# A mixture-of-experts kernel: each expert step branches to one of two product widths, and the overflow branch stands before the first expert

## The chip, the cores and the metric

One core of one Trainium2 chip runs the whole program as a single launch. The metric is the device time of that launch in microseconds (us), and lower is better. Before the change the median of three runs is 975.46 us (975.08 to 977.14).

Engine names are those of the profile: PE is TensorE (matmuls; PEld its weight loads), DVE is VectorE, ACT is ScalarE, POOL is GpSimd, SP is the engine that issues nearly all DMAs.

## What is computed

Three stages follow each other. Only the second is touched by the change, and the start of the third.

```python
x = attention(q, k, v, s)                      # 4 batches, 8 heads, 576 tokens, head size 64 -> x is 2304 x 512
expert = argmax(normed(x) @ normed(emb).T)     # 8 experts
for e in range(8):                             # hidden size 1024
    m = expert == e
    out[m] = gate[m] * (relu(x[m] @ w1[e]) @ w2[e])
y = ((out @ w_a) * (out @ w_b)) @ w_out        # hidden size 1536
```

How many tokens an expert gets depends on the data. All matmuls are made from two parts, a rounded high part and the remainder, so that each product is three matmuls: high by high, low by high, high by low.

## The kernel before, in words

**Attention and routing** (to 260 us of the span). The tokens are scattered by expert into the DRAM tensor `xs`, and the counts are put into a small integer tile `ci`: row 0 the start of each slot, row 1 its count, row 2 the largest excess of a count over the slot's capacity, row 3 the expert that has the slot. Slot 0 is expert 0, slots 1 to 7 the others by falling count. The capacities are fixed: `CAPS = [352, 368, 344, 328, 296, 288, 288, 272]`.

**The expert loop** (267 to 510 us): eight slots `e`, eight steps `f` each. A step takes 128 of the 1024 hidden units. `hmm(e, f)` makes 12 matmuls into a PSUM bank `h` (4 blocks of the model width, 3 parts each); ACT takes the relu and rounds it (`hh`, L1415), DVE makes the remainder (`hl`, L1416). `ymm(e, f)` makes 12 matmuls from `hh` and `hl` into four banks `y`. All of them have `CAPS[e]` columns, whatever the count is. PE runs `hmm` of a step, then `ymm` of the step before, so that ACT and DVE have the length of two groups for `hh` and `hl`. After the last step `y` is copied to SBUF (L173 on ACT, L171 on DVE) and written to `yt`.

Between the steps the same loop issues, in program order:

- `xload(e)`, `xtr(e, d)`: a slot's tokens are loaded and transposed on PE (L1281), rounded on ACT (L1284), the remainder on DVE (L1285);
- `wload2()`, `wsplit2()`: the next expert's weights, 512 KB a load through three staging buffers (SP, L228), rounded on ACT (L258), the remainders on DVE and POOL, one half each (L266). A buffer is free again when both halves are done;
- `zfill(e)`: zeros behind a slot's tokens (SP, L1138); it needs the slot's count in a register of SP (L1259);
- `misc`: five small pieces of the gate's softmax, with two loads of ACT's function table (L1362, L1372);
- in the last expert `tick()`: the third stage's weights, which come as 64-bit numbers, are decoded: on ACT L240, on DVE L241, L248 and L251; then rounded on ACT (L1351) and the remainder made on POOL (L1353). One tick a step, eight in all; the decoding goes on in the third stage.

**Overflow**: if a count is over its capacity, a loop over experts computes the rest in plain fp32. It stands in `tc.If(most > 0)` (L1531), placed before slot 1; `most` is read from `ci` into a register of every engine (L1595) after step 2 of slot 0. Tile closes its hand-written order there and opens it again behind it.

**The third stage** (from 504 us): `abmm`, `omm`; its first items run while the last `ymm` is still open.

The order of the instructions on each engine is the program's order here, by `tc.manual_schedule()`. The engines wait for each other by semaphores alone.

## Time and profile before

| what | value |
|---|---|
| median of 3 runs | 975.46 us |
| the profiled execution | 968.9 us, span of its instructions 967.2 us |
| PE busy | 940.4 us, 97% |
| DVE, ACT, POOL busy | 492.7, 427.8, 337.0 us |
| moved by DMA | 123.30 MB |
| mean granted clock of PE | 0.990 |

The span runs from the first to the last instruction; 1.7 us of the profiled execution lie outside it. Times in rows are microseconds from the start of the span unless "ns" is said. A matmul's record is longer than the distance to the next one, since matmuls overlap in the array; the pace of PE is read from the distance of starts. L-numbers are lines of the kernel before.

### The profile page before, as it was taken

The numbers are of one execution on the slowest core, as the hardware profiler recorded it, in microseconds if no ns is written. First come the engines' busy times: TensorE is split into PE (matmuls) and PEld (weight loads), VectorE is DVE, ScalarE is ACT, GpSimd is POOL, SyncE is SP. The second block draws the span as 40 slices with busy tenths as digits, with TensorE's granted clock in tenths as the row PEclk, the third lists the DMA queues.
The fourth block names the chain that finished last, engine by engine and source line by source line (L and its number), as shares of the span: only waits on it lengthen the run. The fifth ranks groups of instructions, "written<-read, shape, count | busy, mean of one in ns | idle before, by whom it ended". The sixth has DMA issues, their size and how long they took to land.

```text
span 967.2 us, 17807 instructions
## 1 busy us (share of the span) xinstructions
PE 940.4 (97%) x6430; PEld 860.7 (89%) x6431; DVE 492.7 (51%) x1269; ACT 427.8 (44%) x1064; POOL 337.0 (35%) x460
## 2 busy tenths in 40 slices
PE   8999999999799999999999999999999999999996
PEld 7787787877599999999998999999999999999995
DVE  6678787786744433444498888633222222222111
ACT  4588787877463544555454444421211111111111
POOL 8566556579232333334343444552001001001001
PEclk9999999999999999999999999999999999999998
DMA  6789797885285767676575444203010010000000
GB/s 177 191 189 236 177 240 195 186 232 161 91 243 189 214 191 206 204 227 182 181 227 170 156 130 118 80 1 99 1 33 34 1 33 34 1 1 33 1 1 34
DMA packets 107637, 123.30 MB, mean 127 GB/s; under 512 B 59161, under 2 KB 73449, under 8 KB 107545
## 3 DMA queue, kind: packets, MB, share of 16 engines
q1 hardware_dynamic: 103609, 112.37, 41.9%
q0 software_dynamic: 3616, 9.48, 2.7%
q8 instruction: 52, 0.85, 0.4%
q14 instruction: 40, 0.33, 0.1%
q10 hardware_dynamic: 320, 0.27, 0.1%
HBM read 86.58 MB, written 19.92 MB: 110 GB/s over the span
## 4 chain that ended last, share of the span: by engine, by line
issue 32%; PE 26%; DVE 3%; POOL 3%; DMA 2%; ACT 0%; POOLq 0%; SPq 0%; DVEq 0%; ACTq 0%
PE h L1409 9%; PE y L1429 8%; PE h L1469 3%; PE x L1469 3%; PE y L1490 2%; POOL out_dram L1508 1%; POOL pm L1392 1%; DVE cv L248 1%; DMA pm<-pd,pos 1%; DVE cv L251 1%; PE x L1281 1%; DMA st<-in_moe_w_b_dram 0%; PE x L1490 0%; PE h L1490 0%; DVE xl L1457 0%
## 5 line engine op out<-in xcount | busy, mean ns | idle before, releaser
L1480 DVE TENSOR_TENSOR mx<-x,mx 128x384 f32<-128x384 f32 x72 | 40.0, 556 | 222.1 <-PE x L1469 222.0
L1508 POOL DMA_INDIRECT out_dram<-mx,pmt x18 | 17.7, 984 | 290.0 <-DVE mx L1507 221.2
L1481 ACT CAST hh<-mx 128x384 fp32r<-128x384 f32 x71 | 36.4, 513 | 160.5 <-DVE mx L1480 160.5
L1475 ACT COPY mx<-h 128x384 f32<-128x384 f32 x72 | 34.5, 479 | 145.1 <-PE h L1469 145.1
L572 POOL TENSOR_SCALAR bt<-ck,cumc 128x192 f32<-128x192 f32 (+3 forms) x128 | 74.0, 589 | 62.2 <-DVE mn L646 29.5
L652 ACT ACTIVATE z<-z,mn 128x192 f32<-128x192 f32 (+3 forms) x128 | 78.5, 614 | 28.9 <-DVE mn L646 26.4
L1469 PE MATMUL h<-xh,w 128*128 128x384 f32 x288 | 79.8, 337 | 1.0 <-ACT mx L1475 1.0
L1469 PE MATMUL h<-xh,v 128*128 128x384 f32 x288 | 79.7, 337 | 0.0
L1469 PE MATMUL x<-xh,w 128*128 128x384 f32 x288 | 79.0, 334 | 0.0
L266 POOL TENSOR_TENSOR w<-st,w 128x512 fp32r<-128x512 f32 (+1 forms) x41 | 44.1, 1088 | 72.9 <-ACT w L258 55.9
L266 POOL TENSOR_TENSOR v<-st,v 128x512 fp32r<-128x512 f32 x32 | 42.6, 1331 | 73.2 <-ACT v L258 65.7
L646 DVE CUSTOM_DVE_ANT_0 z<-st,bt 128x192 f32<-128x192 f32 (+3 forms) x128 | 59.2, 477 | 16.3 <-PE st L635 11.5
L739 PE MATMUL pt<-ident,z 128*128 128x128 f32 x448 | 65.3, 280 | 1.1 <-DVE ql L385 0.6
L783 PE MATMUL xa<-pT,vn 128*64 128x128 f32 x896 | 65.7, 282 | 0.6
L632 PE MATMUL st<-KS,QS 128*128 128x288 f32 (+3 forms) x160 | 59.6, 378 | 4.8 <-DVE mn L646 2.3
L1409 PE MATMUL h<-xh,w 128*128 128x352 f32 (+3 forms) x256 | 63.3, 316 | 0.0
L1482 DVE TENSOR_TENSOR hl<-mx,hh 128x384 fp32r<-128x384 f32 x71 | 41.0, 577 | 41.1 <-ACT hh L1481 41.1
L1429 PE MATMUL y<-hh,w 128*128 128x352 f32 (+3 forms) x256 | 61.6, 309 | 0.0
L1409 PE MATMUL h<-xh,v 128*128 128x368 f32 (+3 forms) x256 | 61.2, 310 | 0.0
L783 PEld LDWEIGHTS xa<-pT,vn 128*64 128x64 f32 x896 | 47.3, 136 | 14.8 <-issue 5.3
L1429 PE MATMUL y<-hh,v 128*128 128x368 f32 (+3 forms) x256 | 60.1, 306 | 0.0
L1490 PE MATMUL y<-v,hh 128*128 128x512 f32 x192 | 59.8, 392 | 0.0
(286 smaller groups left out, 2545.7 us busy)
## 6 DMA issues: line engine op xcount, KB each, us to landing
st<-in_moe_w_dram SPq DMA_DIRECT2D x64, 512.0 KB, 3.9
ck<-cumd SPq DMA_DIRECT2D x16, 576.0 KB, 5.8
QS<-sp SPq DMA_DIRECT2D x56, 128.0 KB, 4.7
st<-in_moe_w_a_dram SPq DMA_DIRECT2D x12, 512.0 KB, 3.8
st<-in_moe_w_b_dram SPq DMA_DIRECT2D x12, 512.0 KB, 3.6
st<-in_moe_w_out_dram SPq DMA_DIRECT2D x12, 512.0 KB, 3.7
xg<-yt SPq DMA_DIRECT2D x6, 768.0 KB
xg<-xs SPq DMA_DIRECT2D x8, 512.0 KB, 4.8
```

The source lines that it names most:

```text
L266: e.tensor_tensor(out=o[:, 1, a:b], in0=t[:, a:b], in1=o[:, 0, a:b].bitcast(F32), op=ALU.subtract)
L572: nc.gpsimd.tensor_scalar(out=bt[:m, h, :kk], in0=cks[u][:m, h, :kk], scalar1=-1.0, scalar2=cumc[:m, c - 1, hh:hh + 1], op0=ALU.mult, op1= ...
L632: nc.tensor.matmul(st[:m, :wp], lhsT=qs[:, h, s0 - 64:s0 - 64 + m], rhs=ks[:, h, c0:c0 + wp], start=True, stop=False)
L646: nc.vector.tensor_tensor_reduce(out=z[:m, h, c0:c0 + w], in0=st[:m, :w], in1=bt[:m, h, c0:c0 + w], op0=ALU.add, op1=ALU.min, scale=1.0, s ...
L652: nc.scalar.activation(out=z[:m, h, :kk], in_=z[:m, h, :kk], func=AF.Exp, scale=-1.0, bias=m1, accum_out=rsum[:m, tid(b, c), 2 * p + h:2 * ...
L739: nc.tensor.transpose(out=pt[:, 128 * x:128 * x + 128], in_=zs[i][:, h, a0:a0 + 128] if c else z0s[u % 2], identity=ident)
L783: nc.tensor.matmul(xa[64 * h:64 * h + 64, :m], lhsT=v_[:m, 2 * p + h, :], rhs=locs[i][bk, h], start=bk == 0, stop=bk == c,)
L1409: nc.tensor.matmul(ph[:, :CAPS[e]], lhsT=w[:, hl, 128 * f:128 * f + 128], rhs=mv[:, d, :], start=k_ == 0, stop=k_ == 11,)
L1429: nc.tensor.matmul(ys[e][d][:, :CAPS[e]], lhsT=w[:, hl, c0 + 128 * d:c0 + 128 * d + 128], rhs=mv, start=f == 0 and k_ == 0, stop=f == 7 an ...
L1469: nc.tensor.matmul(p, lhsT=w[:, hl, d, c0:c0 + 128], rhs=mv[:, d, :], start=d == 0 and k_ == 0, stop=d == 3 and k_ == 2,)
L1482: nc.vector.tensor_tensor(out=gl, in0=g, in1=gh.bitcast(F32), op=ALU.subtract)
L1490: nc.tensor.matmul(ots[i][t], lhsT=st[:, 128 * t:128 * t + 128], rhs=w[:, hl, c0:c0 + 512], start=f == 0 and k_ == 0, stop=f == 11 and k_ ...
```

## The change

1. A slot has two widths: `ARMS`. PE reads the slot's count into a register (`count`, one load a slot), and every step is now one `tc.If` with two arms, the same 24 matmuls once with the narrow and once with the wide width. `hmm` of a step and `ymm` of the step before stand in the same arm; at a slot's first step and behind its last there is an `If` of 12 matmuls each: nine branches a slot, 72 in all. ACT and DVE go on working on `CAPS[e]` columns.
2. The PSUM banks `h` and `y` are allocated once, not for each step.
3. The overflow branch stands before slot 0, between the load of its tokens and the first `zfill`; its tiles are other buffers, and `w2` is read in halves. The register loads for `zfill(1)` are ahead of it.
4. In the last expert the ticks of steps 4 and 6 are left out, and the remainders of the first six decoded pieces are made on DVE, not on POOL.

```diff
+ARMS = [[288, 352], [352, 368], [336, 344], [312, 328], [280, 296], [256, 288], [256, 288], [256, 272]]
...
-                r = nc.sync.value_load(ci[:1, 1, e:e + 1], min_val=0, max_val=N)
+                r = cbase[e] if e in cbase else nc.sync.value_load(ci[:1, 1, e:e + 1], min_val=0, max_val=N)
...
-                e = nc.gpsimd
+                e = nc.vector if x < 6 else nc.gpsimd
...
+            def count(e):
+                cnts[e] = nc.tensor.value_load(ci[:1, 1, e:e + 1], min_val=0, max_val=N)
+
+            def narrow(e, body):
...
+                    m = len(arms) // 2
+                    with tc.If(cnts[e] < arms[m - 1] + 1) as cmp:
+                        tree(arms[:m])
+                    with cmp.Else():
+                        tree(arms[m:])
...
+                    def both(n):
+                        mm(n)
+                        mm2(n)
+
+                    narrow(e, both)
+                    rest()
...
             xload(0)
+            cbase[1] = nc.sync.value_load(ci[:1, 1, 1:2], min_val=0, max_val=N)
+            who(1)
...
+            for x in range(WARM[2]):
+                warm((hb + yb)[x % 6], w[:, :128], w[:, :512], 1)
+            count(0)
+            most = nc.values_load(ci[:1, 2, 0:1], min_val=-CAP, max_val=N)
+            overflow()
             zfill(1)
...
-                if e == 1:
-                    sched.close()
-                    overflow()
-                    sched.enter_context(tc.manual_schedule())
                 for f in range(8):
-                    hmm(e, f)
-                    if (e, f) == (0, 2):
-                        most = nc.values_load(ci[:1, 2, 0:1], min_val=-CAP, max_val=N)
-                    if prev:
-                        ymm(*prev)
+                    if f == 5 and e + 1 < E:
+                        count(e + 1)
+                    products(e, f, prev)
...
-                        for _ in range(TICKS[0]):
+                        for _ in range(TICKS[0] if f not in (4, 6) else 0):
                             tick()
...
-                    ymm(*prev)
+                    finish(prev)
```

**The order on PE, last expert.** `h` and `y` are PSUM banks, `xh`, `hh` and `hl` the halves of tokens and hidden units, `v` weights. Before, one step follows the other:

```order
L1429 MATMUL y_7779<-hh,v_7575 128x272
L1429 MATMUL y_7779<-hl,v_7575 128x272
L1429 MATMUL y_7779<-hh,v_7575 128x272
L1409 MATMUL h_7804<-xh,v_7413 128x272
L1409 MATMUL h_7804<-xl,v_7413 128x272
```

In the change, the end of the narrow arm of a step, and the start of its wide arm:

```order
L1456 MATMUL y_4965<-hh,v_9020 128x256
L1456 MATMUL y_4965<-hl,v_9020 128x256
L1456 MATMUL y_4965<-hh,v_9020 128x256
L1415 UNCONDITIONAL_BRANCH
L1431 MATMUL h_4960<-xh,v_8625 128x272
L1431 MATMUL h_4960<-xl,v_8625 128x272
```

and the end of that wide arm, with the next step behind it:

```order
L1456 MATMUL y_4965<-hh,v_9020 128x272
L1456 MATMUL y_4965<-hl,v_9020 128x272
L1456 MATMUL y_4965<-hh,v_9020 128x272
L1415 UNCONDITIONAL_BRANCH
L1415 COMPARE_AND_BRANCH
L1431 MATMUL h_4961<-xh,v_8625 128x256
L1431 MATMUL h_4961<-xl,v_8625 128x256
```

The narrow arm comes first, and its last instruction jumps over the 24 matmuls of the wide one. No wait is added at the branches. The other four engines have one unconditional branch for each `If` and nothing else.

**The order on SP, from the load of slot 0's tokens (`xg<-xs`) on.** Before:

```order
L1266 DMA xg<-xs 128x2x512
L1267 DMA xg<-xs 96x512
L1259 TENSOR_LOAD ci
L1259 ISA x2
L1254 TENSOR_LOAD ci
L1254 ISA x2
L1434 TENSOR_LOAD ci
L1434 ISA x2
L1138 ISA
L1138 DMA xs<-zrow 736x1x256
L228 DMA st<-in_moe_w_dram 128x2x512
```

In the change, up to the branch, and from the branch's end:

```order
L1267 DMA xg<-xs 128x2x512
L1268 DMA xg<-xs 96x512
L1627 TENSOR_LOAD ci
L1627 ISA x2
L1255 TENSOR_LOAD ci
L1255 ISA x2
L1635 TENSOR_LOAD ci
L1635 ISA x2
L1580 COMPARE_AND_BRANCH
...
L1580 UNCONDITIONAL_BRANCH
L1139 ISA
L1139 DMA xs<-zrow 736x1x256
```

The number of register loads ahead of the zero fill is the same, three; the branch, with its waits for what SP has issued so far, stands between them and the zero fill, and so ahead of the first weight load.

**The order on DVE, last expert, steps 3 to 5.** `hl` and `xl` are remainders, `cv` the decoded piece, `st` the staging buffer. Before:

```order
L1416 SCALAR_TENSOR_TENSOR hl<-h_7842,hh 128x272
L1457 TENSOR_TENSOR xl<-xg,xh 128x384
L241 TENSOR_SCALAR st_7794<-st_7794 128x512
L248 SCALAR_TENSOR_TENSOR cv<-cv,st_7794 128x512
L251 SCALAR_TENSOR_TENSOR cv<-st_7794,cv 128x512
L1416 SCALAR_TENSOR_TENSOR hl<-h_7885,hh 128x272
L1457 TENSOR_TENSOR xl<-xg,xh 128x384
L241 TENSOR_SCALAR st_7833<-st_7833 128x512
L248 SCALAR_TENSOR_TENSOR cv<-cv,st_7833 128x512
L251 SCALAR_TENSOR_TENSOR cv<-st_7833,cv 128x512
L1416 SCALAR_TENSOR_TENSOR hl<-h_7925,hh 128x272
```

In the change:

```order
L1440 SCALAR_TENSOR_TENSOR hl<-h_4961,hh 128x272
L1508 TENSOR_TENSOR xl<-xg,xh 128x384
L242 TENSOR_SCALAR st_9224<-st_9224 128x512
L1415 UNCONDITIONAL_BRANCH
L1354 TENSOR_TENSOR w_9358<-cv,w_9358 128x512
L249 SCALAR_TENSOR_TENSOR cv<-cv,st_9224 128x512
L252 SCALAR_TENSOR_TENSOR cv<-st_9224,cv 128x512
L1440 SCALAR_TENSOR_TENSOR hl<-h_4960,hh 128x272
L1508 TENSOR_TENSOR xl<-xg,xh 128x384
L1415 UNCONDITIONAL_BRANCH
L1440 SCALAR_TENSOR_TENSOR hl<-h_4961,hh 128x272
```

A tick has one DVE operation more (L1354, the remainder that POOL made), and every second step from step 4 on has no tick.

## Rows read from the trace of the kernel before

**Rows 1.** The page, busy time: share of the span, then instructions.

```profile
PE 940.4 (97%) x6430; PEld 860.7 (89%) x6431; DVE 492.7 (51%) x1269; ACT 427.8 (44%) x1064; POOL 337.0 (35%) x460
```

**Rows 2.** Windows: stretch, length, busy PE, PEld, DVE, ACT, POOL, PE clock, DMA share, GB/s.

```profile
260.00:265.00 5.00, 3.10 (x11) 2.19 (x10) 4.39 (x10) 0.00 (x0) 0.00 (x0) 0.84 0.48 158
265.00:270.00 5.00, 5.00 (x26) 4.74 (x26) 2.04 (x4) 1.84 (x5) 0.00 (x0) 0.67 0.62 125
...
400.00:450.00 50.00, 50.00 (x364) 48.34 (x364) 21.45 (x39) 24.94 (x53) 18.46 (x14) 1.00 0.72 211
```

**Rows 3.** Timeline of PE: start, length, what [idle before and who ended it].

```profile
264.85 2.70 PE L1281 MATMUL y<-ident,xg 128*128 128x128 f32 x12 [1.90 <-DMA xg<-xs]
...
301.79 0.40 PE L1429 MATMUL y<-hl,w 128*128 128x352 f32 x1 [0.30 <-PEq L1531]
...
499.56 0.39 PE L1429 MATMUL y<-hl,v 128*128 128x272 f32 x1 [0.33 <-DVE hl L1416]
...
503.15 0.39 PE L1429 MATMUL y<-hl,v 128*128 128x272 f32 x1 [0.32 <-DVE hl L1416]
...
517.75 0.44 PE L1469 MATMUL h<-xh,w 128*128 128x384 f32 x1 [0.98 <-ACT mx L1475]
```

**Rows 4.** Timeline of PE: firsts of two neighbouring groups of 12 matmuls, two widths.

```profile
298.68 0.33 PE L1409 MATMUL h<-xh,v 128*128 128x368 f32 x1
...
300.69 0.32 PE L1429 MATMUL y<-hh,w 128*128 128x352 f32 x1
...
494.41 0.28 PE L1409 MATMUL h<-xh,v 128*128 128x272 f32 x1
...
495.91 0.29 PE L1429 MATMUL y<-hh,v 128*128 128x272 f32 x1
```

**Rows 5.** Line L1531, the overflow branch (q: an engine's queue).

```profile
L1531 SPq EVENT_SEMAPHORE  x9: 17/17/17, 298.8 to 302.1; - x9
...
L1531 PEldq COMPARE_BRANCH  x1: 357/357/357, 299.1 to 299.1; - x1
```

**Rows 6.** Timeline of PEld: the last weight load ahead of the overflow branch, the first behind.

```profile
300.85 0.34 PEld L1429 LDWEIGHTS y<-hh,w 128*128 128x128 f32 x2
301.75 0.19 PEld L1429 LDWEIGHTS y<-hl,w 128*128 128x128 f32 x1 [0.56 <-issue]
```

**Rows 7.** Line L1595, a register load on PE.

```profile
L1595 PEldq TENSOR_LOAD <-ci x1: 488/488/488, 272.7 to 272.7; - x1
```

**Rows 8.** Groups by line and shape: the shortest matmuls in a row.

```profile
L167 PE MATMUL xa<-ones 128*128 128x128 bf16 x130 | 9.3, 241 | 1.3 <-DVE ones L1068 1.3
```

**Rows 9.** Timeline of ACT, slot 0.

```profile
273.28 1.14 ACT L258 CAST w<-st 128x512 fp32r<-128x512 f32 x2 [2.85 <-DMA st<-in_moe_w_dram]
...
280.62 1.14 ACT L258 CAST v<-st 128x512 fp32r<-128x512 f32 x2 [2.12 <-DMA st<-in_moe_w_dram]
281.78 1.28 ACT L1362 ACT_TABLE_LOAD   x1
...
283.20 0.45 ACT L1415 ACTIVATE hh<-h 128x352 fp32r<-128x352 f32 x1
```

**Rows 10.** Timeline of DVE: slot 0, then the last expert.

```profile
283.73 0.47 DVE L1416 SCALAR_TENSOR_TENSOR hl<-h,hh 128x352 fp32r<-128x352 f32 x1
...
288.12 0.68 DVE L266 TENSOR_TENSOR v<-st,v 128x512 fp32r<-128x512 f32 x1
...
500.41 1.60 DVE L248 SCALAR_TENSOR_TENSOR cv<-cv,st 128x512 uint32<-128x512 uint32 x1
502.05 0.69 DVE L251 SCALAR_TENSOR_TENSOR cv<-st,cv 128x512 uint32<-128x512 uint32 x1
```

**Rows 11.** Timeline of POOL, last expert.

```profile
499.93 1.53 POOL L1353 TENSOR_TENSOR w<-cv,w 128x512 fp32r<-128x512 f32 x1 [2.06 <-issue]
```

**Rows 12.** DMA: queue, packets, MB, share of 16 engines; issue, KB, us to landing.

```profile
q8 instruction: 52, 0.85, 0.4%
...
z<-in_moe_expert_emb_dram POOLq DMA_DIRECT2D x1, 16.0 KB, 2.3
```

More of the change, by code (lines that the diff above doesn't have):

```diff
@@ L1402, in hmm @@
             def hmm(e, f):
[L1403 removed]
+                ph = hb[f % 2]
                 xh, xl = xhs[e]
[L1405 to L1413 removed]
@@ L1414, in hmm, with mm @@
-                hh, hl_ = (hp.tile([128, GT], F32R, name=x)[:, :CAPS[e]] for x in ("hh", "hl"))
-                nc.scalar.activation(out=hh, in_=ph[:, :CAPS[e]], func=AF.Relu)
-                nc.vector.scalar_tensor_tensor(
-                    out=hl_, in0=ph[:, :CAPS[e]], scalar=0.0, in1=hh.bitcast(F32), op0=ALU.max, op1=ALU.subtract
-                )
-                hs[e, f] = (hh, hl_)
+                def mm(n):
+                    k_ = 0
+                    for d in range(4):
+                        w = slots[e, d]
+                        for hl, mv in ((0, xh), (0, xl), (1, xh)):
+                            nc.tensor.matmul(
+                                ph[:, :n], lhsT=w[:, hl, 128 * f:128 * f + 128], rhs=mv[:, d, :n],
+                                start=k_ == 0, stop=k_ == 11,
+                            )
+                            k_ += 1
@@ L1524, in overflow @@
             def overflow():
[L1526 to L1529 removed]
+                xo, xT, *hT = (mxp.tile([128, 512], F32, name="mx") for _ in range(4))
+                w = tmp.tile([128, 512], F32, name="cv").rearrange("p (k c) -> p k c", k=4)
                 po, py = bank("x"), bank("x")
@@ L1572, in overflow @@
-                            nc.vector.tensor_copy(out=yo, in_=py)
+                                for x in range(2):
+                                    nc.sync.dma_start(
+                                        out=w,
+                                        in_=w2[bass.ds(pe, 1), 512 * x:512 * x + 512, 128 * d:128 * d + 128].rearrange("a (k p) c -> p (a k) c", p=128),
+                                    )
+                                    for f in range(4):
+                                        nc.tensor.matmul(
+                                            py[:, 128 * d:128 * d + 128], lhsT=w[:, f, :], rhs=hT[x][:, 128 * f:128 * f + 128],
+                                            start=x + f == 0, stop=x + f == 4,
+                                        )
@@ L1579, in moe_kernel @@
+            who(1)
+            w = slots[0, 0][:, 0, :]
+            hb = [ps.tile([128, 512], F32, name="h%d" % x) for x in range(2)]
+            yb = [ps.tile([128, 512], F32, name="y%d" % x) for x in range(4)]
+            for x in range(WARM[2]):
[3 more added lines that the diff above has]
+            overflow()
             zfill(1)
```

86 lines of the change are left out of this document (44 added, 42 removed).

## Prediction

> **What bounds the kernel now.** I read the page first: PE is busy for 97% of the span [rows 1]. Then the windows, to see where that is not so: PE waits around 255 to 265 us, ahead of the expert loop, and its clock is granted at 0.84 and 0.67 in the windows there [rows 2], which is partly the lower of its two levels, 1.2 GHz; at 400 to 450 us it is busy all the time at full clock, while DVE and ACT are busy for less than half of it. Then PE's timeline from 264 us on: in the whole expert loop and the first items of the third stage only five waits of over 0.2 us are left, 1.90 before slot 0's transposes, 0.30 at the overflow branch, 0.33 and 0.32 in the last expert, 0.98 in the third stage [rows 3]. So the loop is bound by the matmuls' columns, and fewer columns shorten it directly, unless something that is now just in time becomes late.
>
> **The columns.** Groups of 12 matmuls follow each other at 300.69 - 298.68 = 2.01 us with 368 columns and at 495.91 - 494.41 = 1.50 us with 272 [rows 4]: 0.51 us / 12 / 96 = 0.443 ns a column. A slot has 192 such matmuls, so a column is worth 0.085 us a slot. The reference, worked out on its own inputs (seed 0), gives the slots 274, 345, 336, 321, 274, 254, 253 and 247 tokens. The arms are then 288, 352, 336, 328, 280, 256, 256, 256, and the columns saved 64, 16, 8, 0, 16, 32, 32, 16. Slots 1 to 7: 120 x 0.085 = **10.2 us**. Their cover is wide: a step of 24 matmuls with 256 columns still takes 3.0 - 24 x 16 x 0.443 ns = 2.83 us, and weights are split a whole expert ahead of their use.
>
> **Slot 0** would save 64 x 0.085 = 5.4 us, but there PE would run into work that it doesn't pace. In step 3 `hl` is made at 283.73 and takes 0.47 [rows 10], so `ymm` of that step can't start before 284.2. `hl` waits for the relu at 283.20, which stands in ACT's order behind a function table load of 1.28 us, and this behind the rounding of a weight for which ACT sat idle 2.12 us, waiting for its load [rows 9]. That load could be issued only when a staging buffer was free, which hangs on a load that ACT awaited until 273.28 [rows 9]. The chain consists of DMAs; narrower matmuls don't move it. With 288 columns a group takes 1.50 + 12 x 16 x 0.443 ns = 1.59 us, and PE would be at that `ymm` about 8 groups, 12.7 us, after its transposes, so around 281: it waits, and what was saved until then is lost. Behind it eight groups of slot 0 are left: 8 x 12 x 64 x 0.443 ns = 2.7 us. From this I take 0.4 for SP (next part) and 0.3 for the second table load, and add the 0.3 of the overflow branch, which is gone from 301.79 [rows 3]: **2.3 us**. The bounds are 0, if each later step waits in the same way, and 5.4 + 0.3 = 5.7, if none does.
>
> **The branch in front of slot 0.** SP reaches it after as many register loads as before. Its waits include the load of slot 0's tokens, which the zero fill behind it needs anyway. In the trace before, SP took nine short semaphore instructions there, mostly one at a time, 298.8 to 302.1 with a wait in the middle [rows 5]; four or five of them behind that wait are some 0.4 us, by which the zero fill and the first weights are later. That is in the sum above. PE has its register loads and the branch behind the warming matmuls, in the 1.90 us in which it waits for the tokens [rows 3]; ACT, DVE and POOL have nothing to do then. If this cover is too short, PE pays up to 1 us, also because its clock stays low a little longer. I take 0.
>
> **The 72 branches.** Each step now has a compare at its head and a jump at the end of the narrow arm, over 24 matmuls. What a branch costs is seen once: the overflow branch on PE took 357 ns at 299.1 [rows 5]. It was handled far ahead of the array: the weight loads just before it in PE's order ran from 300.85 on, the second of the two at about 301.0 [rows 6], so PE's sequencer is 1.9 us ahead. The 0.56 us without a weight load behind it [rows 6] comes from the waits at that branch's end for PE's own matmuls, and the new branches have none. A register load of 488 ns at 272.7 [rows 7] left no gap either; there are eight of these now. Two branch instructions are 2 x 0.36 = 0.71 us a step, less than 1.9. The lead is also made good within a step: 130 short matmuls ran in 9.3 us, 72 ns each [rows 8], so the sequencer gains at least 24 x (118 - 72) ns = 1.1 us on 256-column matmuls. So I cost the branches at **0**. The bounds are 0, as a branch can't save time, and 72 x 0.71 = 51 us, if the lead hid nothing. The lead is what hides them: where a matmul has to wait for `hh` or `hl`, it is lost, and the next branch shows.
>
> **The last expert.** DVE falls behind there: a decode step took 1.60 us at 500.41, where the like one at 502.05 took 0.69 [rows 10], and POOL's remainder, 499.93 to 501.46, lay beside the long one [rows 11]. Making that remainder on DVE costs 0.68, the price of the same operation on a weight [rows 10], and takes away the 0.9 of that disturbance: a tick becomes some 0.2 shorter on DVE, and steps 4 and 6 have none. Two left-out ticks are late next in the third stage, where each item still has its own one or two and a group of weights is ready an item ahead. The two waits of 0.33 and 0.32 should go, and of the 0.98, which ends with an ACT copy that stands behind two ticks, about two thirds: **1.3 us**, between 0 and 1.6.
>
> **Sum.** 10.2 + 2.3 + 1.3 = 13.8 us. The profiled execution would go from 968.9 to 955.1. The median of the runs, 975.46, is 6.6 above the profiled one; I take the same amount off it: **961.7 us**. A difference of 0.2%, 1.95 us, is about what can be told from no change.
>
> **Rivals.**
> *Slot 0 keeps all of its gain*, because its loads come earlier than I think: 10.2 + 5.7 + 1.6 = 17.5, 958.0 us. Against it stands the 2.12 us wait for a DMA [rows 9]. Chance 0.12.
> *The branches show a little*: the lead is short in steps where `hl` comes late, as in slot 0 and the last expert. With 0.1 us a branch, 7.2 us: 968.9. For it: in the last expert the waits of [rows 3] show that the lead is gone there at times. Chance 0.14.
> *The jump over the unused arm makes PE fetch instructions*: slower. PE's code comes in 52 packets of 0.85 MB together, 16 KB each [rows 12], one for some 247 of the 12,861 matmuls and weight loads [rows 1]. If each jump threw away what had been fetched ahead, PE would wait for a packet in every step: a 16 KB load landed 2.3 us after its issue [rows 12], of which the lead of 1.9 hides most if it is rebuilt, so 0.4 x 72 = 29 us more than forecast, 990.5; if it isn't, up to 2.3 x 72 = 166 us more. It decides from 13.8 / 72 = 0.19 us a branch on. Against it: the jump seen in the trace passed the whole overflow body, 68 matmuls by the code, and cost 357 ns. Chance 0.06.
> The Trainium skill (Runtime: NRT & Kernel Launch, Instruction fetch mechanics) says that a taken branch whose target is outside the two pages of instructions at hand forces a fetch before work can go on, and counts this against run-time control flow. By that rule an estimate is that none of these jumps pays, since 48 instructions are a fifth of the 256 which that page gives for one of its pages, so the target is in the same or the next one: 961.7 again, and the rival's 990.5 only if the next page isn't there yet. The one jump in this trace agrees.
> *The narrow arms aren't taken*, because the counts on the chip are others: only the stalls and the 0.3 go, 1.6 us, 973.9. Slot 2 sits exactly at its arm, 336; one token more costs 0.7 us, the others have room. Chance 0.03.
>
> **Numbers.** My forecast has 0.65. The range 957.0 to 969.5 holds it, the full gain and most of the small branch cost, and takes in the bounds of slot 0 and the last expert; the fetch, the unused arms and a tail of the small cost are left out, about 0.13. Faster by over 0.2%: 0.65 + 0.12 + 0.14 = 0.91; within: 0.03; slower: 0.06.
>
> **What would show it.** In the profile after: first groups of 12 at 1.41 us with 256 columns, no PE wait at the `If` lines; in slot 0 a wait of 1 us or more for `hl` in the first four steps; no wait for `hl` in the last expert; DVE's L249 at 0.7 there, not 1.6; the loop some 12 us shorter. A wait of PE at its own queue in every step, or a matmul pace above 0.118 us in slots 5 to 7, would prove the sum wrong, and so would instruction packets in far greater number than one for 256 passed or skipped instructions.

## The result and the profile after

The changed kernel takes **965.19 us** (median of 4 runs, 962.33 to 968.39), the kernel before 976.3 beside it. The ratio is 0.9886, with a 95% interval of 0.9841 to 0.9931: 11 us less. A repetition on another chip (below) gave 0.9930 (0.9905 to 0.9955), 7 us less. Where the two intervals overlap, 0.9905 to 0.9931, the gain is 7 to 9 us; the forecast had 13.8.

The page of the changed kernel, busy time and PE's instruction queue:

```profile
PE 928.9 (96%) x6430; PEld 847.2 (88%) x6431; DVE 491.8 (51%) x1275; ACT 427.7 (44%) x1064; POOL 328.6 (34%) x454
...
q8 instruction: 65, 1.06, 0.5%
```

PE is busy for 11.5 us less than in [rows 1], yet the profiled execution (968.39 us, span 966.7) is no shorter than the one of before (968.9, span 967.2). SP's timeline shows why that is no contradiction. Kernel before, from the load of slot 0's tokens on:

```profile
261.19 0.37 SPq L1266 DMA_DIRECT2D xg<-xs  x1
...
265.45 0.66 SPq L1138 DMA_DIRECT2D xs<-zrow  x1
266.21 4.15 SPq L228 DMA_DIRECT2D st<-in_moe_w_dram  x3
```

The same in the changed kernel:

```profile
268.03 0.37 SPq L1267 DMA_DIRECT2D xg<-xs  x1
268.45 0.46 SPq L1268 DMA_DIRECT2D xg<-xs  x1
274.57 0.65 SPq L1139 DMA_DIRECT2D xs<-zrow  x1
275.34 4.15 SPq L229 DMA_DIRECT2D st<-in_moe_w_dram  x3
```

This execution reached the token load 6.8 us later. The order on SP ahead of it is unchanged, and in the traces below that load is issued anywhere between 260.1 and 268.0 us (269.5 where the branch is put ahead of it). So two traces are compared **from the token load on**: 967.2 - 261.2 = 706.0 us before, 966.7 - 268.0 = 698.7 after, 7.3 us less. A second fact is in the same rows: the zero fill follows the token load after 4.3 us before and after 6.5 now.

The table gives what each part of that stretch takes: from the token load to slot 1, slots 1 to 6, and from slot 7 to the end. A slot is counted as 192 products in PE's order, from slot 0's first product on. So each boundary lies one group of 12 behind the slot's own first product, 1.4 to 2.0 us later, and a slot's last `ymm` counts with the next slot. The texts put on record before the runs call this boundary a slot's first product.

| kernel | load to slot 1 | slots 1 to 6 | slot 7 to the end | sum |
|---|---|---|---|---|
| before | 39.5 | 180.1 | 486.4 | 706.0 |
| changed, profiled | 38.9 | 171.4 | 488.4 | 698.7 |
| changed, repeated | 38.7 | 171.5 | 485.6 | 695.8 |
| gain, the two | 0.6, 0.8 | 8.7, 8.6 | -2.0, 0.8 | 7.3, 10.2 |
| forecast | 1.7 | 9.3 | 2.8 | 13.8 |

(The forecast's terms are 2.3 for slot 0, 8.8 for the 104 columns of slots 1 to 6 by 0.085, 1.36 for slot 7's 16 columns and 1.3 for the last expert. By the table's boundaries, the 0.3 of the overflow branch at 301.79 and 0.34 for slot 0's last `ymm` pass from slot 0 to the second column; the other shifts are under 0.2.) The middle came to within 0.7 of its forecast; both ends fell short by more. PE's waits of over 0.2 us in the changed kernel, from its timeline, which answer to [rows 3]:

```profile
271.67 0.44 PE L1282 MATMUL y<-ident,xg 128*128 128x128 f32 x2 [1.87 <-DMA xg<-xs]
273.26 1.22 PE L1282 MATMUL y<-ident,xg 96*128 96x96 f32 x10 [1.15 <-DMA xg<-xs]
...
283.76 0.40 PE L1456 MATMUL y<-hh,w 128*128 128x288 f32 x1 [2.32 <-ACT hh L1439]
...
495.39 0.39 PE L1456 MATMUL y<-hl,v 128*128 128x256 f32 x1 [1.72 <-DVE hl L1440]
...
630.44 0.44 PE L1520 MATMUL h<-xh,v 128*128 128x384 f32 x1 [1.07 <-ACT mx L1526]
```

New are the 1.15 behind the first half of slot 0's tokens, the 2.32 in slot 0, the 1.72 in the last expert and the 1.07 far into the third stage. The old 0.33 and 0.32 of the last expert and the 0.98 early in the third stage are gone. None of the waits stands at a branch of L1415.

The 2.32 is a wait for `hh`, which stands on ACT behind the rounding of the first weight that the loop loads:

```profile
282.21 1.14 ACT L259 CAST w<-st 128x512 fp32r<-128x512 f32 x2 [5.11 <-DMA st<-in_moe_w_dram]
283.25 0.46 ACT L1439 ACTIVATE hh<-h 128x352 fp32r<-128x352 f32 x1
```

That rounding starts 14.2 us behind the token load, in the repetition too; before it was 273.28 - 261.19 = 12.1 us [rows 9].

A wait can cost more than itself. Windows around the one of 2.32 (length, busy PE, PEld, DVE, ACT, POOL, PE clock, DMA share, GB/s):

```profile
281.00:285.00 4.00, 1.52 (x10) 1.08 (x9) 1.78 (x3) 2.64 (x5) 1.28 (x1) 1.00 1.03 387
285.00:289.00 4.00, 4.00 (x21) 4.00 (x20) 1.90 (x3) 1.50 (x3) 3.13 (x2) 0.57 0.99 295
289.00:293.00 4.00, 3.89 (x31) 3.66 (x29) 1.69 (x5) 3.71 (x7) 1.30 (x1) 1.00 0.57 199
```

PE idled for 2.3 us, and the granted clock was then 0.57 over the next 4 us: 0.43 / 0.5 x 4 = 3.4 us of them at the lower level of 1.2 GHz. In these 4 us PE handled 21 matmuls where the next window has 31. After the 1.72 in the last expert the same follows (0.69 in 495 to 500). Not every wait has this behind it: after the 1.87 and 1.15 ahead of slot 0 the granted clock was 1.00 from 270 to 280.

Where a stretch at the lower level falls differs between executions of the same kernel. Before, one lay on slot 0's transposes and first products (0.67 in 265 to 270 [rows 2]); in the repetition one lies there as well:

```profile
270.00:275.00 5.00, 5.00 (x29) 4.97 (x30) 2.04 (x4) 2.14 (x5) 0.00 (x0) 0.66 0.43 90
```

In the profiled execution of the changed kernel it was over by then. So the first product stands 6.1 us behind the token load before, 6.2 in the profiled execution and 7.3 in the repetition, although the tokens' second half lands 1.1 to 1.2 us later than before in both, by the DMA landings in the traces.

### The profile page after: what moved, and what is told of

Read it like the earlier page. It is cut to its first block, busy times and chain, and to the rows that moved or that the text cites. A ratio compares the mean times of both kernels' runs of the same rounds, so it can differ in the third digit from the quotient of the medians.

```text
span 966.7 us, 17959 instructions
## 1 busy us (share of the span) xinstructions
PE 928.9 (96%) x6430; PEld 847.2 (88%) x6431; DVE 491.8 (51%) x1275; ACT 427.7 (44%) x1064; POOL 328.6 (34%) x454
## 5 line engine op out<-in xcount | busy, mean ns | idle before, releaser
L1531 DVE TENSOR_TENSOR mx<-x,mx 128x384 f32<-128x384 f32 x72 | 40.0, 555 | 215.1 <-PE x L1520 215.1
L1533 DVE TENSOR_TENSOR hl<-mx,hh 128x384 fp32r<-128x384 f32 x71 | 41.4, 583 | 41.1 <-ACT hh L1532 40.6
L1431 PE MATMUL h<-xh,v 128*128 128x256 f32 (+2 forms) x256 | 60.2, 309 | 0.0
L1456 PE MATMUL y<-hh,w 128*128 128x288 f32 (+3 forms) x256 | 57.0, 298 | 2.3 <-ACT hh L1439 2.3
L1431 PE MATMUL h<-xh,w 128*128 128x288 f32 (+3 forms) x256 | 58.9, 306 | 0.0
L1456 PE MATMUL y<-hh,v 128*128 128x256 f32 (+2 forms) x256 | 58.6, 302 | 0.0
```

The lines of the kernel that those rows point to most:

```text
L1431: nc.tensor.matmul(ph[:, :n], lhsT=w[:, hl, 128 * f:128 * f + 128], rhs=mv[:, d, :n], start=k_ == 0, stop=k_ == 11,)
L1456: nc.tensor.matmul(ys[e][d][:, :n], lhsT=w[:, hl, c0 + 128 * d:c0 + 128 * d + 128], rhs=mv[:, :n], start=f == 0 and k_ == 0, stop=f == 7 a ...
L1533: nc.vector.tensor_tensor(out=gl, in0=g, in1=gh.bitcast(F32), op=ALU.subtract)
```

## The experiments

Theory: the gain is columns; the 72 branches cost nothing; slot 0 lost its part because SP was late, and the last expert because its new waits took back what the old ones gave. Rivals: the branches or PE's instruction fetch cost something; the weights set slot 0 whatever SP does; part 4 of the change simply works or simply doesn't. The table above goes on with the experiments (times of one profiled execution each; the ratio is that of the timed runs to the kernel before on the same chip):

| run | load to slot 1 | slots 1 to 6 | slot 7 to the end | sum | ratio, 95% |
|---|---|---|---|---|---|
| changed kernel again | 38.7 | 171.5 | 485.6 | 695.8 | 0.9930 (0.9905 to 0.9955) |
| fixed widths, no branches | 38.7 | 171.6 | 484.7 | 694.9 | 0.9891 (0.9874 to 0.9908) |
| four times the branches | 41.1 | 171.6 | 485.7 | 698.4 | 0.9908 (0.9878 to 0.9938) |
| both arms wide | 41.2 | 179.6 | 485.8 | 706.5 | 1.0022 (1.0009 to 1.0035) |
| overflow ahead of slot 1 | 39.2 | 171.4 | 485.3 | 695.9 | 0.9925 (0.9908 to 0.9942) |
| overflow ahead of the token load | 36.9 | 171.6 | 485.3 | 693.8 | 0.9940 (0.9918 to 0.9961) |
| zero fill ahead of the overflow | 40.8 | 171.4 | 485.4 | 697.6 | 0.9939 (0.9919 to 0.9958) |
| no overflow | 37.2 | 171.8 | 485.8 | 694.8 | 0.9897 (0.9883 to 0.9911) |
| remainders on POOL | 38.7 | 171.5 | 485.8 | 696.0 | 0.9914 (0.9899 to 0.9929) |
| all ticks | 38.8 | 171.5 | 485.1 | 695.5 | 0.9895 (0.9869 to 0.9922) |
| last expert as before | 39.4 | 171.4 | 486.5 | 697.3 | 0.9923 (0.9910 to 0.9937) |

The ratios of most rows overlap, and the time ahead of the token load varies by several us, so the parts are told apart by the first four columns.

### The branches: none, and four times as many

```diff
-                    with tc.If(cnts[e] < arms[m - 1] + 1) as cmp:
-                        tree(arms[:m])
-                    with cmp.Else():
-                        tree(arms[m:])
+                    tree(arms[:m] if TAKEN[e] <= arms[m - 1] else arms[m:])
```

> The changed kernel without its 72 branches: each slot's products have the width that its arm would have (288, 352, 336, 328, 280, 256, 256, 256), written down as numbers for this input. Theory A (the branches are hidden by PE's lead): the same time as the changed kernel, 965 within 2 us, the same lengths of slots 1 to 6 (31.85, 30.83, 30.88, 27.08, 25.46, 25.31 us) within 0.15 each. Rival B (each branch shows 0.1 us): some 7 us faster, 958, each of these slots 0.9 shorter. Rival C (the fetch of instructions over the jumps slows PE): more than 7 faster, and far fewer instruction packets than 65.

```diff
-                    narrow(e, both)
+                    for m in (mm, mm2):
+                        for x in range(2):
+                            narrow(e, lambda n: m(n, x))
```

(`m(n, x)` makes six of the twelve matmuls; the groups at a slot's ends are split in the same way.)

> The changed kernel with a branch for every 6 matmuls, 256 branches in all instead of 72; the same matmuls in the same order. Theory A (PE's sequencer is so far ahead that branches show nowhere but behind a wait): the slots 1 to 6 keep their lengths within 0.15 us each, the time is the same within 2 us. Rival B (a compare and a jump take 0.34 to 0.7 us of the sequencer, which is the 0.72 us of 6 matmuls, so the lead goes): the slots of 256 columns get 1 to 8 us longer each. Rival C (a fetch at each jump): some tens of us.

(Chips differ: the kernel before took 968.1 us beside the first of these and 973.4 beside the second, so the ratios and the lengths are to be compared.) Without branches slots 1 to 6 take 171.6 us, with them 171.4 and 171.5, with 256 in place of 72 again 171.6. **Theory A in both**, for these slots. PE's branch instructions, first of the changed kernel, then of the one with four times as many (durations: least, median, most, in ns):

```profile
L1415 PEldq COMPARE_BRANCH  x135: 65/169/335, 273.5 to 507.2; - x135
```

```profile
L1415 PEldq COMPARE_BRANCH  x480: 65/169/412, 272.9 to 506.5; - x160
```

The 135 are a compare for each of the 72 `If`s and a jump behind each narrow arm taken (slot 3 takes the wide one). Two of 0.17 us fit even beside 6 matmuls of 0.12 us each, if PE's sequencer is as far ahead of the array as the prediction read from [rows 6]. PE's instruction packets are 52 with fixed widths and 65 with branches: 13 more of 16 KB. By the count that the prediction made (one packet for some 247 instructions), the unused arms, 8 x (7 x 48 + 2 x 24) = 3072 instructions, are 12.4 packets; they are fetched, and nothing waits for them. In slot 0 the kernel with 256 branches was 2.4 us longer; PE waited there 1.24 and 2.02 us for `hh`. Whether the branches have a share in that is not settled, since such waits differ between executions. The last expert leaves the same question open: slot 7 takes 27.4 us without branches, with no wait of PE over 0.2 us, and 28.0 to 28.6 in eight of the table's kernels that have them (the other two undo the columns or the new last expert). On one chip the kernel without branches took 957.1 us, two with them 959.6 and 960.1 ("remainders on POOL" and "overflow ahead of slot 1"). Some 0.6 us there may be the price of branches in steps where `hl` comes late, as one of the prediction's rivals had it, or chance: no run repeats it.

### The columns: both arms wide, and far fewer columns

```diff
-                        tree(arms[:m])
+                        tree(arms[m:])
```

> The changed kernel with the wide width in both arms: all branches are there, no column is saved. Theory A (the gain is columns alone): slots 1 to 6 take 33.4, 31.5, 30.9, 28.5, 27.6, 27.4 us again, 8.5 us more in all; in slots 0 and 7 the waits for hh and hl shrink as PE gets there later, so these take 1 us more at most; 974 to 975 us, within 2 of the kernel before. Rival (the move of the overflow branch or the branches bring a gain of their own): under 971.

This kernel takes 970.0 us, ratio 1.0022: without its saved columns the change is 2 us slower than the kernel before. Against the fixed widths on the same chip (957.1 us) the columns are worth 12.9 us; from the token load on it is 706.5 - 694.9 = 11.6 us, of which 2.5 lie in slot 0, 8.0 in slots 1 to 6 and 1.1 in slot 7. In sum, all of the gain is columns. The first stretch is 1.7 us longer than before here, with the same columns: what the moved branch costs in this execution. Slots 1 to 6 are 0.5 us shorter than before, also with the same columns: slot 1 no longer has the overflow branch and its wait of 0.30 [rows 3].

The second question is how far fewer columns go on paying. Slots 5 and 6, down from 288 columns to 256, gave 2.2 us each and not 2.6.

```diff
-                tree(ARMS[e])
+                body(192)
```

(on top of the fixed widths)

> The changed kernel without its 72 branches and with 192 columns in all products of the slots (all tokens of a slot beyond 192 are left out of the products). Theory A (a matmul can't follow the one before it faster than the weights are loaded, 119 to 120 ns, so that columns under some 256 save nothing): matmuls follow each other at 118 to 120 ns, slots 1 to 6 take 25.0 to 25.4 us each. Rival B (0.443 ns a column goes on): 90 ns, 19.5 us for such a slot, unless the weights' loads and rounding become the bound, some 20 to 22 us with waits for v and w on PE.

The firsts of two neighbouring groups of 12 matmuls, changed kernel with 256 columns:

```profile
429.08 0.28 PE L1431 MATMUL h<-xh,v 128*128 128x256 f32 x1
...
430.52 0.28 PE L1456 MATMUL y<-hh,v 128*128 128x256 f32 x1
```

and with 192:

```profile
403.98 0.28 PE L1454 MATMUL y<-hh,v 128*128 128x192 f32 x1
...
405.32 0.28 PE L1429 MATMUL h<-xh,v 128*128 128x192 f32 x1
```

1.44 us and 1.34 us, so 120 and 112 ns a matmul, where 0.443 ns a column gave 118 and 90. Both theories missed: the pace goes on falling below 256 columns, but slowly. Between [rows 4] and here the pace is 168 ns at 368 columns, 125 at 272, 120 at 256, 112 at 192: from 272 down a column saves 0.3 ns, from 256 down 0.13. Slots 2 to 6 took 22.7 to 24.1 us, transposes included, and the kernel, which leaves tokens out, 932.5 us in its single run. PE had no wait of over 0.2 us in slots 3 to 5, so neither the loads from DRAM nor the rounding of the weights set this pace. The Trainium skill (TensorE: Matmul & The Clock Gate, LDWEIGHTS (loading the stationary operand)) gives a weight load as its columns divided by 1.2, in ns; an estimate by it is 107 ns for the 128 columns here. The 112 ns fit a pace set by the weight loads within 5 ns. No run here varied their size, so this cause is argued, not shown.

### The overflow branch: four places, and none

```diff
             for e in range(E):
+                if e == 1:
+                    overflow()
                 for f in range(8):
...
-            overflow()
             zfill(1)
```

> The changed kernel with the overflow branch back ahead of slot 1. Theory A (SP stands at the branch until the second half of slot 0's tokens has landed, so zero fill and weight loads are issued 2.3 us later than before, and PE pays for it in slot 0): the zero fill comes 4 to 4.5 us after the token load instead of 6.5, the wait of 2.32 for hh shrinks to under 1 and the half-clock stretch behind it goes, slot 0 takes 30.0 to 31.0 us instead of 32.64, minus 0.3 for the branch ahead of slot 1: 962 to 964. Rival B (the weights land when they do, whatever SP does): the wait stays over 2 us, 965 to 966.

```diff
-            xload(0)
             cbase[1] = nc.sync.value_load(ci[:1, 1, 1:2], min_val=0, max_val=N)
...
             overflow()
+            xload(0)
             zfill(1)
```

> The changed kernel with the overflow branch ahead of the load of slot 0's tokens, instead of behind it. Theory A (the jump makes PE fetch 16 KB of instructions, which stand in one DMA queue ahead of the last rows of that load; and SP can't leave the branch before all it has issued has landed): the tokens land 3.5 us after their issue instead of 5.2, the zero fill is issued 4 to 4.5 us behind the token load instead of 6.5, slot 0's first products start 5.0 us behind it instead of 6.2; the waits for hh in slot 0 are 1 us each or less; from the token load to the end 693.5 to 695, 1.5 to 2 less than the changed kernel, if the token load itself is not issued later. Rival B (the weights set slot 0 by themselves): the same as the changed kernel within 0.5 us. Rival C (SP reaches the token load later, since it now waits at the branch for the counts): token load to end as in A, but the time 1 us longer.

```diff
-            overflow()
             zfill(1)
             wload2()
             wload2()
+            overflow()
```

> The changed kernel with the zero fill and the first two weight loads of slot 1 ahead of the overflow branch; the token load stays ahead of them, and the branch stays ahead of slot 0's products. Theory A (SP's taken jump over the overflow loop costs it 2.1 us, as its next instructions have to be fetched, whether anything is in flight or not; in the run with the branch ahead of the token load SP stood 2.7 us there with nothing of its own in flight): the zero fill is issued 4.0 to 4.6 us behind the token load instead of 6.5, SP stands 2 us at the branch behind the loads, and from the token load to slot 1's first product it is 37.3 to 38.2 us instead of 38.7 to 38.9; 694.5 to 695.5 us from the token load to the end. Rival B (SP waits at the branch for all that it has issued): it stands there 5 us or more, and slot 0 is longer than 39 us.

```diff
-            overflow()
             zfill(1)
```

> The changed kernel without the overflow branch (its part of the computation is left out; no count of this input is over its capacity). Theory A (the branch costs slot 0 SP's 2.1 us and, by PE's fetch of 16 KB in one DMA queue, 1.1 us of the token load): the tokens land 3.5 us behind their issue, zero fill 4.0 to 4.6, first product 5.0; from the token load to slot 1's first product 37.0 to 37.6 us, 1.3 to 1.8 less than with the branch, and no more, since the waits for hh behind the weight loads of 1 us each stay. Rival B (the branch is the whole loss of slot 0 against its 5.7 us): 34 to 35 us.

What the line of the branch (L1580) shows on SP and on PE, changed kernel first: duration in ns, then the first and last start in us. The nine semaphore instructions stand behind SP's jump.

```profile
L1580 SPq EVENT_SEMAPHORE  x9: 17/17/17, 273.5 to 274.1; - x9
...
L1580 PEldq COMPARE_BRANCH  x1: 368/368/368, 268.3 to 268.3; - x1
...
L1580 SPq COMPARE_BRANCH  x1: 50/50/50, 271.3 to 271.3; - x1
```

Ahead of the token load:

```profile
L1580 SPq EVENT_SEMAPHORE  x9: 17/17/17, 268.5 to 269.1; - x9
...
L1580 SPq COMPARE_BRANCH  x1: 50/50/50, 265.8 to 265.8; - x1
```

Behind zero fill and weight loads (SP's branch at 270.9):

```profile
L1580 SPq EVENT_SEMAPHORE  x9: 17/17/17, 271.4 to 275.6; - x9
```

Ahead of slot 1:

```profile
L1580 SPq EVENT_SEMAPHORE  x9: 17/17/17, 300.6 to 301.2; - x9
...
L1580 PEldq COMPARE_BRANCH  x1: 3667/3667/3667, 293.8 to 293.8; - x1
...
L1580 SPq COMPARE_BRANCH  x1: 53/53/53, 296.3 to 296.3; - x1
```

Two different waits stand at this branch. The first lies between the jump and the first semaphore instruction: 2.2 us in the changed kernel, 2.7 ahead of the token load, 4.3 ahead of slot 1, but 0.5 behind the zero fill, and 0.5 in the kernel before, whose semaphore instructions begin at 298.8 [rows 5] behind this jump:

```profile
L1531 SPq COMPARE_BRANCH  x1: 53/53/53, 298.3 to 298.3; - x1
```

Ahead of the token load SP had no tokens, zero fill or weights of this stage in flight to wait for. Nor is it a wait of the first semaphore instruction: in the trace's semaphore events that one counts SP's own register loads, and the last of these was through at 270.7 in the changed kernel, ahead of the jump. In the three cases with the long wait the DMA trace has an instruction packet of the second instruction queue (q14) within it, in the two with 0.5 none. But such a packet also stands 3.9 us behind the token load in the kernel before and in the one without overflow, which have no branch there, so the packet alone doesn't prove that the jump asked for it. On PE the same jump took 357 ns before, 368 now, and **3667** ahead of slot 1, with a packet of PE's instructions (q8) within it, and PE stood still for 1.87 us:

```profile
297.95 0.42 PE L1431 MATMUL h<-xh,v 128*128 128x352 f32 x1 [1.87 <-PEq L1580]
```

So the same taken jump over the overflow loop costs SP 0.5 us in two kernels and 2 to 4 us in others. That the long ones wait for instructions to be fetched is argued: no other wait is seen that lasts as long, but no run here forces a fetch. The Trainium skill (Runtime: NRT & Kernel Launch, Instruction fetch mechanics) says that a taken branch to a target outside the two pages of instructions at hand has to wait for a fetch; these rows fit that, with 53 + 470 ns against 50 + 2110 on SP and 0.36 us against 3.67 on PE. Which of the two it is changed with the branch's place: in the nine traces that have it where the change has it, SP's pause was 2.1 to 2.4 us each time.

The second wait lies among the nine semaphore instructions: behind the zero fill they last from 271.4 to 275.6, as SP waits for what it has issued. Rival B was nearer there: the third weight load came late, and it is 40.8 us to slot 1. The zero fill, now ahead of the branch, still came 5.3 us behind the token load and not 4.0 to 4.6, since it waits for the tokens, and these landed at 5.2. So of the 2.3 us by which the change delays the zero fill (4.3 to 6.5) some 1.1 are the late tokens, and only the other 1.2 are SP's branch.

The price of the branch is seen without it. The waits of PE in slot 0, no overflow:

```profile
265.27 1.72 PE L1282 MATMUL y<-ident,xg 128*128 128x128 f32 x12 [0.73 <-DMA xg<-xs]
274.99 0.40 PE L1456 MATMUL y<-hh,w 128*128 128x288 f32 x1 [1.03 <-ACT hh L1439]
...
279.37 0.40 PE L1456 MATMUL y<-hh,w 128*128 128x288 f32 x1 [0.53 <-ACT hh L1439]
...
284.35 0.40 PE L1456 MATMUL y<-hh,w 128*128 128x288 f32 x1 [0.79 <-ACT hh L1439]
```

The tokens come in one piece, the first products start 5.1 us behind the token load and not 6.2 or 7.3, ACT's first weight comes after 11.8 us and not 14.2, and slot 1 is reached after 37.2 us and not 38.9 or 38.7: **the branch costs some 1.5 us where it stands now**, one execution against two. The rest of slot 0's 5.7 us stays lost: three waits for `hh` behind ACT's rounding of late weights remain. Theory A held. Part of the 1.5 is the token load itself. In the changed kernel the DMA view of 268.9 to 273 has one packet of PE's instructions among the 384 of that load:

```profile
q1 hardware_dynamic: 384, 0.72, 49.2%
q8 instruction: 1, 0.02, 1.3%
```

Without the overflow there is none in the like window, and with the branch ahead of slot 1 neither; in both the second half of the tokens isn't late. By the landings in the traces this goes for all of them: in the eight with such a packet 2.6 to 2.8 us behind the load's issue, the last of the second half's 16 landings comes 1.1 to 1.3 us behind the other 15; in the three without a packet, the kernel before among them, 0.1 at most. That the packet holds up the rows behind it is a close match, not a proof.

The place ahead of the token load gives the shortest sum, 693.8, but there SP's 2.7 us and its semaphores come before the load is issued (269.5), and the ratio, 0.9940, is not better, as Rival C had it. Ahead of slot 1 Theory A held for slot 0's start: the zero fill came after 4.1 us and the waits for `hh` were 1.00 and 1.17. But PE's 1.87 at the jump takes it back: 39.2 - 1.87 = 37.3 us, as without the overflow. No place that was tried beats the change's own by more than the measurement's uncertainty.

### The last expert

The changed kernel once more, without an edit:

> The changed kernel itself once more, beside the others of this call. Theory A (the wait of 1.72 for hl in the last expert belongs to the one execution: SP's issue of the third stage's first load took 2.06 us there and only 0.64 in the run with the fixed widths, and the tokens came late): slot 7 takes 27.4 to 28.5 us, no wait over 0.6 us in it, and from the load of slot 0's tokens to the end it is 695 to 697 us, some 10 less than the 706.0 of the kernel before; ratio of the times 0.989 to 0.992. Rival B (it belongs to the branches, as the fixed widths don't have it): slot 7 over 30 us, 698 to 700 us.

```diff
-                e = nc.vector if x < 6 else nc.gpsimd
+                e = nc.gpsimd
```

> The changed kernel with all remainders of the decoded pieces on POOL again, the ticks of steps 4 and 6 still left out. Theory A (the wait of 1.72 for hl in the last expert comes from DVE's remainder, which waits 0.86 for ACT's rounding, and that behind ACT's own wait of 2.21 for the third stage's first tokens): the wait for hl falls to under 1 us and slot 7 takes 29.5 to 30.5 us instead of 31.20; 963.5 to 965. Rival B (only ACT's wait for the tokens makes it, DVE's place does not matter): slot 7 stays at 31.2 within 0.3. Rival C (POOL beside DVE disturbs, 0.9 us a tick): slot 7 over 31.5.

```diff
-                        for _ in range(TICKS[0] if f not in (4, 6) else 0):
+                        for _ in range(TICKS[0]):
```

> The changed kernel with the ticks of steps 4 and 6 of the last expert back; the remainders stay on DVE. Theory A (the wait of 1.07 at 629 us, in the third stage, is the two left-out ticks, paid there): that wait is gone, and slot 7 takes 0.3 to 0.8 us more than in the changed kernel's undisturbed run, as hl stands behind 2.4 us of decoding in every step: same time within 0.8. Rival B (the 1.07 comes from DVE's remainders or from elsewhere): it stays.

Both of these edits together:

> The changed kernel with its fourth part undone as a whole: the ticks of steps 4 and 6 are back and all remainders of the decoded pieces are on POOL, as in the kernel before. Theory A (this part gains nothing: what it takes off the last expert it pays back in the third stage, 1.07 us at 629): slot 7 takes 28.1 to 28.9 us (29.42 of the kernel before less some 1.0 for 16 columns), with waits for hl as before it; the wait at 629 is gone and one of 0.6 to 1.0 stands early in the third stage; from slot 7's first product to the end 485.0 to 485.6 us, against 485.63 in the repetition of the changed kernel. Rival B (the part gains 1.3 us, as forecast): 486.6 to 487.0 us there, the time 1.3 us longer than the changed kernel's.

In the repetition the wait of 1.72 is one of 0.98, and slot 7 takes 28.4 us instead of 31.2; the other kernels with this last expert have 27.4 to 28.6. So Theory A holds in its main point: the size of the wait belongs to the execution. (Its bound of 0.6 us did not hold.) The chain of the profiled execution, on SP, ACT and DVE:

```profile
482.28 2.06 SPq L1500 DMA_DIRECT2D xg<-yt  x1
```

```profile
490.34 0.51 ACT L1507 CAST xh<-xg 128x384 fp32r<-128x384 f32 x1 [2.21 <-DMA xg<-yt]
491.72 0.69 ACT L241 ACTIVATE cv<-st 128x512 f32<-128x512 f32 x1 [0.87 <-DMA st<-in_moe_w_b_dram]
492.31 0.62 ACT L1352 CAST w<-cv 128x512 fp32r<-128x512 f32 x1
```

```profile
492.96 0.69 DVE L1354 TENSOR_TENSOR w<-cv,w 128x512 fp32r<-128x512 f32 x1 [0.86 <-ACT w L1352]
493.57 0.68 DVE L249 SCALAR_TENSOR_TENSOR cv<-cv,st 128x512 uint32<-128x512 uint32 x1
494.29 0.69 DVE L252 SCALAR_TENSOR_TENSOR cv<-st,cv 128x512 uint32<-128x512 uint32 x1
494.90 0.43 DVE L1440 SCALAR_TENSOR_TENSOR hl<-h,hh 128x272 fp32r<-128x272 f32 x1
```

The issue of the third stage's first tokens took SP 2.06 us (0.64 in the kernel with fixed widths, 1.73 in the repetition). ACT waits 2.21 for them, its decode and its rounding (L1352) are late, and DVE's remainder (L1354), which is new there, waits 0.86 for that rounding. The rest of the tick and then `hl` stand behind it. POOL used to do this wait. SP's slow issue only makes the chain longer: without the overflow the issue took 0.65, and still ACT waited 1.27 for the tokens, DVE 0.87 for the rounding and PE 1.01 for `hl`. DVE's L249 now takes 0.69 where L248 took 1.60 [rows 10]. In the two kernels below that give POOL its remainders back, L249 or L252 takes 1.60 to 1.78 again in each tick that has POOL's L1354 beside it, and no other does, as the prediction had it.

Both halves of part 4 are seen by themselves. With POOL's remainders slot 7 is 28.0 us, no longer than with DVE's (28.1 to 28.6 in the other kernels with branches), and not 29.5 to 30.5 as Theory A had it, which took the profiled execution's 31.2 for its base; the third stage has a wait of 0.57 at its start. With all ticks the wait of 1.07 at 629 us is gone, as Theory A said, and one of 0.64 stands early in the third stage:

```profile
511.20 0.45 PE L1520 MATMUL h<-xh,w 128*128 128x384 f32 x1 [0.64 <-ACT mx L1526]
```

The slot is 28.5 us long then, 0.1 more than in the repetition and not 0.3 to 0.8. Against the change neither is worth more than 0.5 us in the sum. Both undone, slot 7 to the end takes 486.5 us, within a tenth of Rival B's forecast and against Theory A: by this one execution part 4 is worth 0.7 to 1.2 us against the 485.3 to 485.8 of most kernels above that keep it (484.7 with fixed widths, 488.4 in the profiled execution). The old waits are back, on columns that are 16 fewer:

```profile
487.31 0.39 PE L1456 MATMUL y<-hl,v 128*128 128x256 f32 x1 [0.53 <-DVE hl L1440]
490.90 0.38 PE L1456 MATMUL y<-hl,v 128*128 128x256 f32 x1 [0.45 <-DVE hl L1440]
494.49 0.39 PE L1456 MATMUL y<-hl,v 128*128 128x256 f32 x1 [0.46 <-DVE hl L1440]
...
508.92 0.44 PE L1520 MATMUL h<-xh,w 128*128 128x384 f32 x1 [1.01 <-ACT mx L1526]
```

Slot 7 takes 29.5 us in this kernel with 256 columns, as long as the 29.4 with 272 before: DVE sets its length there, and the columns bring nothing.

## Why the prediction was right, and where not

The sign and the main term were right: 965.19 lies in the range, and the gain is columns. The forecast of 961.7 was too low; 3.6 of the 13.8 us did not come in the repetition's trace, 6.5 in the profiled one.

- **The columns of slots 1 to 6**: 9.3 forecast by the table's boundaries, 8.6 and 8.7 measured. The groups of 12 with 256 columns take 1.44 us, not 1.41: from 288 to 256 columns slots 5 and 6 gave 0.8 us less together than forecast, as below 272 columns the pace no longer falls by 0.443 ns a column. By the prediction's own sign, a pace above 0.118 us in slots 5 to 7 (0.120 measured), this term of the sum was wrong. Slot 1 came as forecast, 1.8 of 1.9, with the 0.3 of the overflow branch in it.
- **The columns of slot 7**: 1.36 forecast as part of the 10.2, though the prediction itself had DVE falling behind there. Measured: nothing with the old last expert, and with the new one 28.0 to 28.6 us mostly against 28.7 with the wide arms, some 0.1 to 0.7.
- **Slot 0**: 1.7 forecast for the table's first stretch, 0.6 and 0.8 measured. The mechanism was right: PE waits behind ACT's rounding of late weights, though for `hh` and not `hl`, and already at the `ymm` of step 1, two steps earlier than forecast. Without the overflow branch the stretch gains 39.5 - 37.2 = 2.3 us. That this is the forecast's figure for slot 0 is luck: the forecast has 0.4 off it for SP's part, which isn't there without the branch, and 1.0 of the 2.3 is the earlier first product (5.1 against 6.1 us), as the 12 transposes ran at full clock (1.72 against 2.70 us). The step that failed is **"four or five of them behind that wait are some 0.4 us"**, SP's part: the zero fill, and the weights behind it, came 2.3 us later. Some 1.2 of it is the branch on SP, where the jump's own pause of 2.1 us had no row for the new place, and 1.1 the late second half of the tokens. With the same late tokens the step "I take 0" for the transition failed in the repetition, by 1.3 us at a clock like the one before; in the profiled execution the full clock at the transposes hid it but for 0.2. The bound "up to 1 us" was there.
- **The branches at 0**: right, and with room, in slots 1 to 6, where 256 cost no more; in slots 0 and 7 a small price is not ruled out. The rivals of 0.1 us a branch and of a fetch in every step fell, and the estimate from the Trainium skill's page, that none of these jumps pays, held. But a jump can cost microseconds. It showed at the one jump over a large body, on SP in the change's own place and on PE ahead of slot 1. The prediction's evidence against it, one jump of 357 ns, was one sample of two possible outcomes.
- **The last expert**: 1.3 forecast, 0.7 to 1.2 by undoing it, and in the profiled execution a loss. L249 at 0.69 and the 0.98 (now under 0.2) came as forecast. Wrong was "two left-out ticks are late next in the third stage, where ... a group of weights is ready an item ahead": they cost 1.07 at 629 us, far into the third stage. Also wrong was "no wait for `hl` in the last expert": DVE's new operation was costed by its 0.68 alone and not by what it waits for, ACT's rounding.
- **From one execution to the median**: the 6.6 us between them were carried over as they were. The traces show that the token load alone is issued anywhere within 8 us (260.1 to 268.0), in kernels that don't differ ahead of it. How much of that the two ratios hold is not known.

## What to carry to other kernels

A run-time branch around whole groups of matmuls can be free on TensorE, at one every 6 matmuls even, while the array has no wait; what it costs behind one is not settled here. Fewer columns then pay in full down to some 272 columns here, and little below 256. A jump over a large body is another matter: price it on every engine that takes it, above all on the one that issues the DMAs, at its short and at its long price. Where an operation moves to another engine, count what it waits for and what then stands behind that wait, not its duration alone; and compare traces from a common event behind the part that isn't changed.

## What was not expected of the hardware

- The same taken jump took SP 0.5 or 2.2 us and more, and PE 0.36 or 3.67 us, by where it stood. That the difference is whether its next instructions were at hand is argued.
- Matmuls of 128 x 128 weights in fp32r follow each other at 112 ns with 192 columns and at 120 with 256, where 0.443 ns a column would make 90 and 118.
- One 16 KB packet of instructions within a load of 704 KB goes with a last landing 1.1 to 1.3 us behind the others, in all eight traces that have it there.
- The same DVE operation on integers (L249, L252) takes 0.69 us alone and 1.60 to 1.85 where POOL's remainder runs beside it: one of the two in each such tick, before and in the two kernels that give POOL its remainders back.
- A wait of 2.3 us on PE was followed by some 3 us at the lower clock; the one of 1.72 as well. Those of 0.5 to 1.3 in slot 0 of the repetition and of the run without overflow were not (1.00 in windows of 5 us from 275 to 295 in both), and neither were the 1.87 and 1.15 ahead of slot 0 in the profiled execution.
